# Block-causal attention with a gated convolution FFN: P's transposes read float32r instead of float32, through a second tile that takes over P's bytes, and the planned slot is 10.65 instead of 10.91

## The chip, the cores and the metric

The kernel runs on one core of one Trainium2 chip. The metric is the device time of one execution in microseconds (us), as the median of several runs. The profile is one further execution of the same program, recorded by the hardware profiler; its span runs from the first to the last recorded instruction.

Engines are named as the profile names them: PE is the matrix engine, PEld its weight loads (they run beside PE), DVE the vector engine, ACT the scalar engine, POOL the GpSimd engine, SP the engine that issues most DMAs.

## The reference

Eight sequences of 576 tokens, eight heads of 64 dimensions. Attention is causal by blocks of 64 tokens; its output feeds a feed-forward layer whose hidden values are gated by a convolution over three tokens.

```python
scores = (1/8) * q @ k.T                       # per batch and head, 576 x 576
scores = where(block(i) >= block(j), scores, -1e9)    # blocks of 64
attn = exp(scores - max) ; attn /= sum(attn) + 1e-9
x = concat over heads of attn @ v              # (8, 576, 512)
h = maximum(x @ w_in, 0)                       # (8, 576, 1024)
c[s] = w0*h[s-1] + w1*h[s] + w2*h[s+1]         # per channel
out = (h * sigmoid(c)) @ w_out                 # (8, 576, 512)
```

## The kernel before

**Numbers.** Nearly all matrix products are made with float32r operands, a rounded float32, in three passes: each operand is split into a high part (its rounding) and a low part (the rest), and high by high, high by low and low by high are added in PSUM. Transposes on PE are the exception: they take plain float32 and a float32 identity, `ident`, and only what is evicted from PSUM is split.

**Attention.** Heads go in pairs ("visits"). Batch 0 is visited twice per pair, part A for tokens 0 to 255 and part B for 256 to 575; batches 1 to 7 in one visit per pair, 28 visits in all, part `None`. A visit has two slots, one for each head. For a block of 128 query rows, `stage_s` makes the scores (L930, L932 on PE), the maximum on DVE (L940), the exponential on ACT with its sum (L943), and `finish` the reciprocal on DVE and the normalisation on POOL (`norm`, L859), which multiplies the tile `p0` to `p4` in place by the reciprocal. Parts A and B have their own copies of `norm` (L1072, L1012). The tiles have the widths 128, 256, 384, 512 and 576, two buffers each, and one buffer for `p4`, the last 64 rows of both heads.

**P's transposes.** P stands with queries on the partitions and P times V needs keys there, so `stage_x` transposes P in pieces of 128 columns on PE (`tr` in `one_bank`, L1116): the piece of P is the stationary operand, loaded as weights, and the identity moves through the array. Each call of `one_bank` fills one PSUM bank (`w`) with one to four pieces; ACT evicts the high part (L1126, `ptah` or `ptbh`), DVE the low part (L1129, `ptal` or `ptbl`). In a visit of part `None` there are eight calls with 3, 3, 4, 3, 3, 4, 4 and 1 pieces: 25 transposes. Part A has 2 calls with 3 pieces, part B 6 calls with 19 pieces in all. Together 28 x 25 + 4 x 6 + 4 x 19 = 800 transposes. P times V follows at L1207. Q's and K's transposes (L725) are float32 too.

**FFN.** `ffn` multiplies x by w_in (L1283), runs the convolution and the gate on ACT, DVE and POOL, and multiplies by w_out (L1342). Its matmuls are "paced": they have target times and are laid between the attention work of the next batch.

**The order.** No loop order reaches the engines. The kernel first writes all pieces of work as `Op`s, each with engine, estimated duration, dependencies, buffers and a target time. `Plan.order` then simulates the five engines and fixes the order in which each engine gets its instructions; at run time every engine follows its fixed list and waits on semaphores. Target times of the attention work come from the length of a slot, `SLOT`, 10.91 us in the part `None`; `ffn` takes its pace from `H * SLOT / 2`. A group of n transposes is put at n x 0.109 + 0.003 us. Where the simulated PE would idle longer than a limit, the planner lays in matmuls that compute nothing (`work`, L1473: identity by identity, 512 columns, into a PSUM bank that is free).

Of the kernel before, what the change touches and what calls it, by code (L numbers as in the profile page):

```python
# [9 lines left out]
F32 = mybir.dt.float32  # L10
F32R = mybir.dt.float32r
# [222 lines left out]
def kernel(  # L234
# [10 lines left out]
    nc = tc.nc  # L245
# [81 lines left out]
    def one(shape, dtype, tag):  # L327
        return pl.buf(cp, shape, dtype, tag, 1)
# [514 lines left out]
    def finish(blocks, st, c0, t0, pb, done, exps, part):  # L843
        a, b_, w_ = c0 + blocks[0], c0 + blocks[-1] + 1, 2 if blocks[0] < 4 else 3

        def i1():
            x = 4 if blocks[0] == 4 else 4 + 2 * blocks[0]
            nc.vector.tensor_reduce(out=st.ap[:, a:b_],
                                    in_=st.ap[:, x:x + w_ * (b_ - a)].rearrange("p (n w) -> p n w", w=w_),
                                    op=ALU.add, axis=AX.X)  # L850

        def i2():
            nc.vector.reciprocal(st.ap[:, a:b_], st.ap[:, a:b_])  # L853

        o = pl.op(DVE, 0.15, i1, t0, deps=exps[4] if blocks[0] == 4 else [exps[x] for x in blocks], bufs=[st])
        o = pl.op(DVE, 0.12, i2, t0, deps=[o], bufs=[st])
        for x in blocks:
            def norm(pt=pb[x], col=c0 + x):
                nc.gpsimd.tensor_scalar(out=pt.ap, in0=pt.ap, scalar1=st.ap[:, col:col + 1], scalar2=0.0,  # L859
                                        op0=ALU.mult, op1=ALU.add)  # L860

            w = 128 * (x + 1) if x < 4 else S
            if x in NORMS[part]:
                def norm_a(pt=pb[x], col=c0 + x):
                    nc.scalar.activation(out=pt.ap, in_=pt.ap, func=AF.Copy, scale=st.ap[:, col:col + 1])

                done[x] = pl.op(ACT, c_act(w, False, True), norm_a, t0 + 0.3, deps=[o], bufs=[st, pb[x]])
                continue
            done[x] = pl.op(POOL, c_pool(w) + 0.08, norm, t0 + 0.3, deps=[o], bufs=[st, pb[x]])


    def last_s(t, ready4, t0, pb, done, exps, part):
        st4 = keep([P, 16], F32, "st4", 2, EPS)
        p4 = one([P, S], F32, "p4")
        pb[4] = p4
        ms, es, banks = [], [], []
        for j in range(2):
            k0, k1 = HS * j, HS * j + HS
            sb = bank("s")
            banks.append(sb)  # L880

            def mm4(sb=sb, k0=k0, k1=k1):
                qdh, qdl = t["qz"].ap[:, S - 64:S + 64], t["qdl"].ap
                for n, (q_, k_) in enumerate(((qdh, "kh"), (qdl, "kh"), (qdh, "kl"))):
                    nc.tensor.matmul(sb.ap[:, 0:HS], q_, t[k_].ap[:, k0:k1], start=(n == 0), stop=(n == 2))  # L885

            def mx4(sb=sb, j=j):
                nc.vector.tensor_reduce(out=st4.ap[:, j:j + 1], in_=sb.ap[:, 0:HS], op=ALU.max, axis=AX.X)

            o = pl.op(PE, 3 * c_mm(HS), mm4, t0, deps=ready4, bufs=[sb, t["qz"], t["qdl"], t["kh"], t["kl"]])  # L890
            ms.append(pl.op(DVE, c_dve(HS), mx4, t0 + 0.3, deps=[o], bufs=[sb, st4]))

        def mm4b():
            nc.vector.tensor_reduce(out=st4.ap[:, 2:3], in_=st4.ap[:, 0:2], op=ALU.max, axis=AX.X, negate=True)
# [12 lines left out]

    def stage_s(ops, hh, at, part, shared):
# [52 lines left out]
    def stage_sb(ops, at):  # L961
# [4 lines left out]
        for z, i in enumerate((2, 3)):  # L966
# [16 lines left out]
                      area=0.85, rows64=True)  # L983
            es = []
            for hh in range(2):
                pt = two([P, nk], F32, f"p{i}")
                pb[hh][i] = pt
                j = 2 * z + hh

# [19 lines left out]
            o = pl.op(DVE, 0.13, i2, t0 + 1.2 + OSH, deps=[o], bufs=[st])  # L1009
            for hh in range(2):  # L1010
                def norm(pt=pb[hh][i], col=12 + 2 * z + hh):
                    nc.gpsimd.tensor_scalar(out=pt.ap, in0=pt.ap, scalar1=st.ap[:, col:col + 1], scalar2=0.0,  # L1012
                                            op0=ALU.mult, op1=ALU.add)

                done[hh][i] = pl.op(POOL, c_pool(nk) + 0.08, norm, t0 + 1.5 + OSH + 0.3 * hh, deps=[o], bufs=[st, pb[hh][i]])
        last_s(t, ready4, at + OSB * 2, pb[0], done[0], exps[0], "B")
# [4 lines left out]
    def stage_sa(ops, at):  # L1021
# [1 line left out]

        st = keep([P, 16], F32, "st", 4, EPS)
        sb = [bank("s"), bank("f")]
        pb = [{i: two([P, 128 * (i + 1)], F32, f"p{i}") for i in range(2)} for _ in range(2)]
        done, exps = [{}, {}], []

        def mm(tiles):
# [24 lines left out]
        def ex(hh, i):  # L1054
            def go():
                j = 2 * hh + i
                nc.scalar.activation(out=pb[hh][i].ap, in_=sb[hh].ap[:, 128 * i:128 + 256 * i], func=AF.Exp,
                                     bias=st.ap[:, j:j + 1], accum_out=st.ap[:, 4 + 2 * j:5 + 2 * j])

            return go  # L1060
# [8 lines left out]
        def norm(hh, i):  # L1069
            def go():  # L1070
                j = 12 + 2 * hh + i
                nc.gpsimd.tensor_scalar(out=pb[hh][i].ap, in0=pb[hh][i].ap, scalar1=st.ap[:, j:j + 1], scalar2=0.0,  # L1072
                                        op0=ALU.mult, op1=ALU.add)

            return go

# [23 lines left out]
    def stage_x(pbd, hh, at, part, shared):  # L1100
# [10 lines left out]
        def one_bank(trs, rows, n, hi, lo, deps, t0, bufs_p, bufs_hi, bufs_lo, sub_ok, tag, shape):  # L1111
            tb = bank(tag)

            def tr():
                for z, (x, c, kk, col) in enumerate(trs):
                    nc.tensor.matmul(tb.ap[0:kk, col:col + P], pb[x].ap[:, 128 * c:128 * c + kk], ident,  # L1116
                                     start=(z == 0), stop=True, is_transpose=True, skip_group_check=True)
# [392 lines left out]
```

## Time and profile before

| what | value |
|---|---|
| time, median of 3 runs (lowest to highest) | 806.87 us (806.38 to 807.34) |
| span of the profiled execution | 805.2 us |
| PE busy | 793.4 us, 99% of the span |
| weight loads busy | 712.1 us, 88% |
| DVE, ACT, POOL busy | 649.9, 614.6, 424.1 us |
| granted PE clock, mean | 1.000 |
| P's transposes (L1116): matmuls busy | 125.0 us, 800 of them |
| P's normalisation on POOL (L859): busy | 140.4 us, 256 of them |

The profiled execution has no time of its own beside its span; the median of the runs is 1.7 us above the span, which is what lies ahead of the first and behind the last instruction. Matmuls are recorded from issue to end and overlap each other, so that the recorded mean of one (274 ns for a transpose) is a latency; what one costs PE is the distance to the next.

### The profile page before, as it was taken

The page shows a single profiled execution, that of the slowest core. Times are in us where ns is not written, and L with a number is a line of the kernel's source. Part 1 is how long each engine was busy: PE and PEld are TensorE (multiplying, and loading weights), DVE is VectorE, ACT ScalarE, POOL GpSimd, SP SyncE. Part 2 cuts the span into 40 slices and gives each one's busy share as a digit, 9 for nine tenths or more (in the row PEclk, how much of TensorE's full clock was granted, in tenths as well). Part 3 has the DMA queues.
Part 4 walks back from the last instruction along what each step waited for, and adds up shares of the span by engine and source line. Part 5 has one row for each costly group of instructions (what it writes and reads, how often), then busy time and mean ns, then how long its engine had stood idle before and what let it go on. Part 6 is the DMA issues. An engine that isn't in the chain of part 4 may idle for free.

```text
span 805.2 us, 17261 instructions
## 1 busy us (share of the span) xinstructions
PE 793.4 (99%) x5381; PEld 712.1 (88%) x5381; DVE 649.9 (81%) x1889; ACT 614.6 (76%) x1769; POOL 424.1 (53%) x607
## 2 busy tenths in 40 slices
PE   8999999999999999999999999999999999999998
PEld 5668889888989899898989889898989989899996
DVE  6898989988979779797988869798887959887541
ACT  4769978977968769796978769697877858787652
POOL 3345556666655446565555645555455635546431
PEclk9999999999999999999999999999999999999999
DMA  9423556475445545444455544445554434540001
GB/s 231 143 65 92 144 122 149 111 182 145 104 116 125 134 118 120 110 101 120 120 135 135 122 117 99 102 115 135 135 122 118 110 98 105 136 105 14 14 27 40
DMA packets 163327, 91.35 MB, mean 113 GB/s; under 512 B 134540, under 2 KB 138660, under 8 KB 163236
## 3 DMA queue, kind: packets, MB, share of 16 engines
q1 hardware_dynamic: 162692, 90.12, 45.1%
q8 instruction: 44, 0.72, 0.4%
q14 instruction: 47, 0.39, 0.2%
q10 hardware_dynamic: 544, 0.13, 0.1%
HBM read 38.30 MB, written 9.44 MB: 59 GB/s over the span
## 4 chain that ended last, share of the span: by engine, by line
PE 82%; ACT 6%; DVE 5%; DMA 2%; issue 2%; POOL 2%; SPq 1%; ACTq 0%; POOLq 0%; DVEq 0%
PE f L1283 21%; PE f L1342 19%; PE w L1207 10%; PE w L1116 9%; PE s L930 4%; PE s L932 4%; PE w L1342 3%; PE s L885 3%; PE w L725 3%; PE s L1283 2%; ACT ptbh L1126 1%; DMA vn<-in_v_dram 1%; POOL vv L437 1%; DMA gh<-in_moe_w_in_dram 1%; PE s L1473 1%
## 5 line engine op out<-in xcount | busy, mean ns | idle before, releaser
L859 POOL TENSOR_SCALAR p<-p,st 128x256 f32<-128x256 f32 (+4 forms) x256 | 140.4, 562 | 139.0 <-DVE st L853 82.8
L1323 POOL TENSOR_TENSOR gl<-t,gh 128x288 fp32r<-128x288 f32 (+2 forms) x128 | 104.1, 816 | 148.8 <-ACT gh L1320 145.4
L943 ACT ACTIVATE p<-s,st 128x128 f32<-128x128 f32 x224 | 118.0, 527 | 41.9 <-DVE st L940 40.8
L1116 PE MATMUL w<-ident,p 128*128 128x128 f32 (+1 forms) x800 | 125.0, 274 | 0.7 <-DVE xl L1231 0.3
L940 DVE TENSOR_REDUCE st<-s 128x1 f32<-128x128 f32 x224 | 107.5, 484 | 3.4
L1126 ACT ACTIVATE ptbh<-w 128x384 fp32r<-128x384 f32 (+1 forms) x192 | 93.7, 508 | 21.7 <-PE w L1116 19.2
L1116 PEld LDWEIGHTS w<-ident,p 128*128 128x128 f32 (+1 forms) x800 | 95.0, 139 | 15.5 <-POOL p L859 1.7
L1342 PE MATMUL f<-woh,gh 128*128 128x512 f32 x248 | 103.9, 419 | 0.0
L1283 PE MATMUL f<-xh,wih 128*128 128x290 f32 (+2 forms) x480 | 97.7, 307 | 0.3 <-DVE t L1316 0.3
L1342 PE MATMUL f<-woh,gl 128*128 128x512 f32 x248 | 97.9, 395 | 0.0
L1129 DVE TENSOR_TENSOR ptbl<-w,ptbh 128x512 fp32r<-128x512 f32 (+1 forms) x144 | 89.6, 633 | 10.3 <-ACT ptbh L1126 7.4
L1342 PE MATMUL f<-wol,gh 128*128 128x512 f32 x248 | 97.7, 394 | 0.0
L1283 PE MATMUL f<-xh,wil 128*128 128x290 f32 (+2 forms) x480 | 94.5, 304 | 0.0
L1283 PE MATMUL f<-xl,wih 128*128 128x290 f32 (+2 forms) x480 | 93.3, 304 | 0.0
L1304 DVE SCALAR_TENSOR_TENSOR t<-f,cw,t 128x287 f32<-128x287 f32 (+3 forms) x120 | 59.9, 499 | 19.0 <-ACT t L1300 17.3
L1283 PEld LDWEIGHTS f<-xh,wih 128*128 128x128 f32 x480 | 73.1, 189 | 1.9 <-DVE t L1316 0.5
L1283 PEld LDWEIGHTS f<-xl,wih 128*128 128x128 f32 x480 | 72.9, 189 | 1.0
L1283 PEld LDWEIGHTS f<-xh,wil 128*128 128x128 f32 x480 | 73.2, 189 | 0.4
L932 PE MATMUL s<-kl,qz 128*128 128x128 f32 x224 | 72.1, 322 | 0.0
L1320 ACT ACTIVATE gh<-t 128x288 fp32r<-128x288 f32 (+2 forms) x128 | 56.7, 445 | 8.3 <-DVE t L1316 7.4
L1300 ACT ACTIVATE t<-f,cw 128x288 f32<-128x288 f32 (+2 forms) x120 | 59.9, 499 | 3.8
L1308 DVE SCALAR_TENSOR_TENSOR t<-f,cw,t 128x288 f32<-128x288 f32 (+3 forms) x120 | 60.6, 505 | 1.3
(230 smaller groups left out, 2001.0 us busy)
## 6 DMA issues: line engine op xcount, KB each, us to landing
out_dram<-stage SPq DMA_DIRECT2D x36, 256.0 KB, 2.2
vn<-in_v_dram SPq DMA_DIRECT2D x64, 128.0 KB, 2.9
qn<-in_q_dram SPq DMA_DIRECT2D x56, 144.0 KB, 2.9
kn<-in_k_dram SPq DMA_DIRECT2D x56, 144.0 KB, 3.1
ka<-kh SPq DMA_DIRECT2D x56, 144.0 KB, 2.6
kb<-kh SPq DMA_DIRECT2D x56, 144.0 KB, 2.6
qa<-qh SPq DMA_DIRECT2D x28, 144.0 KB, 2.4
qb<-qh SPq DMA_DIRECT2D x28, 144.0 KB, 2.6
```

Of the source, the lines that this page charges most:

```text
L859: nc.gpsimd.tensor_scalar(out=pt.ap, in0=pt.ap, scalar1=st.ap[:, col:col + 1], scalar2=0.0, op0=ALU.mult, op1=ALU.add)
L932: nc.tensor.matmul(sb.ap[:, 0:nk], qz.ap[:, z:z + 128], kl.ap[:, 0:nk], start=False, stop=True)
L940: nc.vector.tensor_reduce(out=st.ap[:, i:i + 1], in_=sb.ap[:, 0:nk], op=ALU.max, axis=AX.X, negate=True)
L943: nc.scalar.activation(out=pt.ap[:, 0:nk], in_=sb.ap[:, 0:nk], func=AF.Exp, bias=st.ap[:, i:i + 1], accum_out=st.ap[:, 4 + 2 * i:5 + 2 * i])
L1116: nc.tensor.matmul(tb.ap[0:kk, col:col + P], pb[x].ap[:, 128 * c:128 * c + kk], ident, start=(z == 0), stop=True, is_transpose=True, skip_ ...
L1126: nc.scalar.activation(out=hi(), in_=src(), func=AF.Copy)
L1129: nc.vector.tensor_tensor(out=lo(), in0=src(), in1=hi(), op=ALU.subtract)
L1207: nc.tensor.matmul(tb.ap[0:m, q0 - qa:qb - qa], vv.ap[:, chunk(c), hh, w[ps_]], pm.ap[:, 128 * c + q0:128 * c + qb] if qa == 0 else pm.ap[ ...
L1283: nc.tensor.matmul(fb.ap[:, 0:n2], wt[:, c, fs], xs[c][xi].ap[:, x0:x0 + n2], start=(n + c - c0 == 0), stop=(n + c - c0 == 3 * NCC - 1))
L1308: nc.vector.scalar_tensor_tensor(out=t.ap[:, 0:i1], in0=fb.ap[:, own + 1:own + 1 + i1], scalar=cw[:, 2 * NFC + f:2 * NFC + f + 1], in1=t.a ...
L1323: nc.gpsimd.tensor_tensor(out=gbuf[1].ap[:, f, carry:carry + no], in0=t.ap[:, 0:no], in1=gbuf[0].ap[:, f, carry:carry + no], op=ALU.subtract)
L1342: nc.tensor.matmul(fb.ap[:, 0:DM], gbuf[a].ap[:, f, cs], w[:, f, :], start=(f == 0 and n == 0), stop=(f == NFC - 1 and n == 2))
```

## The change

The identity that P's transposes move is now `rident`, the float32r copy that was there already, and P is read as float32r. P itself is still written as float32 by ACT and normalised as float32 by POOL. A new class, `Twin`, holds two tiles under one tag with one buffer: the float32 tile, and a float32r tile that is allocated in the same place once the float32 tile is done with. So that the second tile has a writer, each tile is two columns wider, and a GpSimd memset (`turn`) writes zeros into the two last columns of the float32r tile; the transposes are made to depend on that memset by hand. The two buffers of a tag are now two tags of one buffer each. The bytes that the transposes read are the ones that the normalisation wrote. There is one memset for each normalisation: 28 x 9 + 4 x 4 + 4 x 5 = 288.

The planner's figures change with it: a group of n transposes is put at n x 0.088 + 0.003 us (with `area=0.6` in place of 0.49, the share by which it counts as PE activity), and `SLOT` is 10.65. The memset is not among the planner's `Op`s; it stands in the function of the normalisation.

```diff
+class Twin(Buf):
+    def __init__(self, pool, shape, tag):
+        super().__init__(pool, shape, F32, tag)
+        self.r = None
+
+    @property
+    def raw(self):
+        if self.r is None:
+            pool, shape, _, tag = self.args
+            self.r = pool.tile(shape, F32R, tag=tag, name=tag + "r")
+        return self.r
+
+    def turn(self, nc):
+        n = self.args[1][1]
+        self.set = nc.gpsimd.memset(self.raw[:, n - 2:n].bitcast(F32), 0.0)
...
-    SLOT, SLOTA, SLOTB = 10.91, 3.29, 6.01
+    SLOT, SLOTA, SLOTB = 10.65, 3.29, 6.01
...
+    def twin(nk, tag, n):
+        hist = pl.tags.setdefault(tag, [])
+        b = Twin(cp, [P, nk + 2], f"{tag}{len(hist) % n}")
+        hist.append(b)
+        if len(hist) > n:
+            b.before = hist[-1 - n]
+        return b
...
             def norm(pt=pb[x], col=c0 + x):
-                nc.gpsimd.tensor_scalar(out=pt.ap, in0=pt.ap, scalar1=st.ap[:, col:col + 1], scalar2=0.0,
+                x = pt.ap[:, 0:pt.args[1][1] - 2]
+                nc.gpsimd.tensor_scalar(out=x, in0=x, scalar1=st.ap[:, col:col + 1], scalar2=0.0,
                                         op0=ALU.mult, op1=ALU.add)
+                pt.turn(nc)
...
-            pt = two([P, nk], F32, f"p{i}")
+            pt = twin(nk, f"p{i}_", 2)
...
             def tr():
                 for z, (x, c, kk, col) in enumerate(trs):
-                    nc.tensor.matmul(tb.ap[0:kk, col:col + P], pb[x].ap[:, 128 * c:128 * c + kk], ident,
+                    m = nc.tensor.matmul(tb.ap[0:kk, col:col + P].bitcast(F32R), pb[x].raw[:, 128 * c:128 * c + kk], rident,
                                      start=(z == 0), stop=True, is_transpose=True, skip_group_check=True)
-
-            o = pl.op(PE, len(trs) * 0.109 + 0.003, tr, t0, deps=deps, bufs=[tb] + bufs_p, area=0.49)
+                    tc.add_manual_dep(m.ins, pb[x].set.ins.name, mybir.DependencyInfo(mybir.DependencyClass.Sync, mybir.DependencyReason.DATA), reason="values")
+
+            o = pl.op(PE, len(trs) * 0.088 + 0.003, tr, t0, deps=deps, bufs=[tb] + bufs_p, area=0.6)
```

The same two lines of `norm` stand in `stage_sb` and `stage_sa`. Since the planner's figures changed, each engine's whole order is another. In the rows below a row is line, operation, output<-inputs and size of the output, and xN counts equal neighbours. The lines of the changed kernel stand some 30 further down: L859 is L887 there, L930 and L932 are L959 and L961, L1116 is L1149, L1283 is L1317, L1342 is L1376, L1473 is L1507; the memset is L57.

POOL, one head of a visit in the middle of the program, with buffer numbers; before, four normalisations with one subtraction of the FFN (`gl`) between them, then V's split (`vv`) and the normalisation of `p4`:

```order
L859 TENSOR_SCALAR p0_5526<-p0_5526,st2_101 128x128
L859 TENSOR_SCALAR p1_5549<-p1_5549,st2_101 128x256
L859 TENSOR_SCALAR p2_5565<-p2_5565,st2_101 128x384
L1323 TENSOR_TENSOR gl_1022<-t_5545,gh_1017 128x288
L859 TENSOR_SCALAR p3_5599<-p3_5599,st2_101 128x512
L395 TENSOR_SCALAR vv_5641<-vn_5276 128x10x64
L437 TENSOR_TENSOR vv_5641<-vn_5276,vv_5641 128x10x64
L859 TENSOR_SCALAR p4_5643<-p4_5643,st41_111 128x576
```

The same engine in the changed kernel, at about the same place:

```order
L887 TENSOR_SCALAR p4_0_5935<-p4_0_5935,st41_111 128x576
L57 MEMSET p4_0r_5985 128x2
L422 TENSOR_SCALAR xh_6003<-xt_5744 128x576
L1357 TENSOR_TENSOR gl_1007<-t_5871,gh_998 128x288
L1411 TENSOR_TENSOR xl_6034<-xt_5744,xh_6003 128x576
L1357 TENSOR_TENSOR gl_1007<-t_5960,gh_998 128x288
L887 TENSOR_SCALAR p0_1_5990<-p0_1_5990,st3_103 128x128
L57 MEMSET p0_1r_6114 128x2
L887 TENSOR_SCALAR p1_1_6047<-p1_1_6047,st3_103 128x256
L57 MEMSET p1_1r_6118 128x2
L887 TENSOR_SCALAR p2_1_6085<-p2_1_6085,st3_103 128x384
L57 MEMSET p2_1r_6127 128x2
```

Behind each normalisation stands its memset, which waits for the normalisation's end by a semaphore of POOL itself; transposes wait for the memset.

PE, second half of a slot in the middle of the program; before, scores of 384 and 512 columns, P's transposes and FFN matmuls (`f<-xh,wih` and so on) in turn:

```order
L932 MATMUL s<-kl,qz_105 128x384
L1116 MATMUL w<-ident,p_5903 128x128
L1116 MATMUL w<-ident,p_5910 128x128 x2
L1283 MATMUL f<-xh,wih 128x290 x2
L725 MATMUL w<-ident,kn 128x96 x3
L1283 MATMUL f<-xh,wih 128x290 x2
L930 MATMUL s<-kb,qb 128x512
L932 MATMUL s<-kl,qz_105 128x512
L1116 MATMUL w<-ident,p_5927 128x128 x3
L1283 MATMUL f<-xh,wil 128x290 x2
L1116 MATMUL w<-ident,p_5974 128x128 x4
```

The same place in the changed kernel:

```order
L961 MATMUL s<-kl,qz_105 128x384
L752 MATMUL w<-ident,kn 128x96 x3
L1317 MATMUL f<-xh,wih 128x290 x2
L1149 MATMUL w<-rident,p_0r 128x128 x3
L752 MATMUL w<-ident,kn 128x96 x3
L1317 MATMUL f<-xh,wih 128x290 x2
L959 MATMUL s<-kb,qb 128x512
L961 MATMUL s<-kl,qz_105 128x512
L1149 MATMUL w<-rident,p_0r 128x128 x3
L1317 MATMUL f<-xh,wil 128x290 x4
L1317 MATMUL f<-xl,wih 128x290 x2
L1149 MATMUL w<-rident,p_0r 128x128 x8
```

The transposes keep their place among scores and FFN matmuls, but the groups fall together otherwise: here eight stand in one run where before a run had four.

PE in part B of batch 0, where the planner lays in matmuls that compute nothing; before, four and three of them (`f<-rident`, `w<-rident`):

```order
L1116 MATMUL w<-ident,p_1183 128x128 x3
L1132 MATMUL w<-ptbh,nident 128x512
L1283 MATMUL f<-xl,wih 128x256 x4
L1116 MATMUL w<-ident,p_1368 128x128 x4
L1132 MATMUL w<-ptbh,nident 128x384
L1473 MATMUL f<-rident 128x512 x4
L1116 MATMUL w<-ident,p_1368 64x128
L1473 MATMUL w<-rident 128x512 x3
L1116 MATMUL w<-ident,p_1218 128x128 x3
```

The changed kernel there:

```order
L1149 MATMUL w<-rident,p_0r 128x128 x3
L1166 MATMUL w<-ptbh,nident 128x512
L1317 MATMUL f<-xl,wih 128x256 x4
L1149 MATMUL w<-rident,p_0r 128x128 x4
L1166 MATMUL w<-ptbh,nident 128x384
L1507 MATMUL f<-rident 128x512 x3
L1149 MATMUL w<-rident,p_0r 64x128
L1507 MATMUL s<-rident 128x512 x5
L1149 MATMUL w<-rident,p_1r 128x128 x3
```

Over the whole program there are 117 such matmuls in place of 100, all but four of the 117 ahead of the end of part B.

More of the change, by code (lines that the diff above doesn't have):

```diff
@@ L873, in last_s @@
         st4 = keep([P, 16], F32, "st4", 2, EPS)
-        p4 = one([P, S], F32, "p4")
+        p4 = twin(S, "p4_", 1)
         pb[4] = p4
@@ L985, in stage_sb @@
             for hh in range(2):
-                pt = two([P, nk], F32, f"p{i}")
+                pt = twin(nk, f"p{i}_", 2)
                 pb[hh][i] = pt
@@ L1025, in stage_sa @@
         sb = [bank("s"), bank("f")]
-        pb = [{i: two([P, 128 * (i + 1)], F32, f"p{i}") for i in range(2)} for _ in range(2)]
+        pb = [{i: twin(128 * (i + 1), f"p{i}_", 2) for i in range(2)} for _ in range(2)]
         done, exps = [{}, {}], []
@@ L1056, in go @@
                 j = 2 * hh + i
-                nc.scalar.activation(out=pb[hh][i].ap, in_=sb[hh].ap[:, 128 * i:128 + 256 * i], func=AF.Exp,
+                nc.scalar.activation(out=pb[hh][i].ap[:, 0:128 * (i + 1)], in_=sb[hh].ap[:, 128 * i:128 + 256 * i], func=AF.Exp,
                                      bias=st.ap[:, j:j + 1], accum_out=st.ap[:, 4 + 2 * j:5 + 2 * j])
@@ L1071, in go @@
                 j = 12 + 2 * hh + i
-                nc.gpsimd.tensor_scalar(out=pb[hh][i].ap, in0=pb[hh][i].ap, scalar1=st.ap[:, j:j + 1], scalar2=0.0,
+                x = pb[hh][i].ap[:, 0:128 * (i + 1)]
+                nc.gpsimd.tensor_scalar(out=x, in0=x, scalar1=st.ap[:, j:j + 1], scalar2=0.0,
                                         op0=ALU.mult, op1=ALU.add)
+                pb[hh][i].turn(nc)
             return go
```

4 lines of the change are left out of this document (3 added, 1 removed).

## The prediction

> **What bounds the kernel now.** I read the page's busy times first, then the stretches of the span, then the chain that ended last, then the single weight loads.
>
> ```profile
> span 805.2 us, 17261 instructions
> PE 793.4 (99%) x5381; PEld 712.1 (88%) x5381; DVE 649.9 (81%) x1889; ACT 614.6 (76%) x1769; POOL 424.1 (53%) x607
> ```
>
> A busy PE is not yet a full PE, so the stretches count more. Each row: stretch, its length, then busy us of PE, weight loads, DVE, ACT and POOL.
>
> ```profile
> core 0: us, PE busy (x) PEld busy (x) DVE busy (x) ACT busy (x) POOL busy (x), PEclk, DMA share, GB/s
> 60.00:130.00 70.00, 69.37 (x514) 60.69 (x513) 62.12 (x179) 62.56 (x178) 39.17 (x62) 1.00 0.51 129
> 250.00:400.00 150.00, 149.84 (x1043) 138.33 (x1042) 126.00 (x371) 118.52 (x345) 80.78 (x114) 1.00 0.47 115
> 400.00:550.00 150.00, 149.85 (x1038) 137.71 (x1037) 126.01 (x371) 119.17 (x349) 83.59 (x115) 1.00 0.49 119
> ```
>
> From 60 us on PE is never free for more than about 1% (69.37 of 70), in the middle for 0.1% (149.84 of 150), at the full granted clock, while DVE has 16% to spare. So PE is the bound, and what a matmul costs there is its distance to the next one. The chain that ended last gives that distance for the transposes: start, length, what.
>
> ```profile
> 502.47 0.69 PE f L1342 x3
> 503.16 0.87 PE w L1116 x8
> 504.74 0.11 PE w L1116
> ```
>
> Eight transposes hold PE for 0.87 us, a single one for 0.11: **0.109 us each**, twice what 128 moving columns need elsewhere. A 512-column float32r matmul follows the one before it after 0.23 and 0.22 us, so that 128 such columns take 0.225 / 4 = 0.056 us:
>
> ```profile
> 405.95 0.39 PE L1342 MATMUL f<-woh,gh 128*128 128x512 f32 x1
> 406.18 0.39 PE L1342 MATMUL f<-wol,gh 128*128 128x512 f32 x1
> 406.40 0.40 PE L1342 MATMUL f<-woh,gl 128*128 128x512 f32 x1
> ```
>
> With weights it is the other way round. Mean length of one load is the number behind the comma; the 128x128 and 128x64 in each row are the weights.
>
> ```profile
> L1116 PEld LDWEIGHTS w<-ident,p 128*128 128x128 f32 x768 | 91.9, 140 | 15.1 <-POOL p L859 1.7 <-POOL p L1072 1.0 <-DVE ptbl L1129 0.8
> L1116 PEld LDWEIGHTS w<-ident,p 128*64 128x64 f32 x32 | 3.5, 111 | 0.4
> L1283 PEld LDWEIGHTS f<-xh,wih 128*128 128x128 f32 x480 | 73.1, 189 | 1.9 <-DVE t L1316 0.5 <-DVE st L894 0.2
> L1207 PEld LDWEIGHTS w<-ptbl,vv 128*64 128x64 f32 x256 | 26.8, 136 | 0.9
> ```
>
> Going from 64 to 128 columns adds 140 - 111 = 29 ns to a transpose's float32 load and 189 - 136 = 53 ns to a float32r load. So 128 columns take about 0.058 us in the first and 0.106 us in the second, the rest is fixed. Where float32r matmuls are short, their loads pace them: here three loads start 0.11 us apart, behind matmuls of 128 columns.
>
> ```profile
> 401.25 0.19 PEld L930 LDWEIGHTS s<-kb,qb 128*128 128x128 f32 x1
> 401.36 0.19 PEld L932 LDWEIGHTS s<-kl,qz 128*128 128x128 f32 x1
> 401.47 0.30 PEld L1283 LDWEIGHTS f<-xl,wih 128*128 128x128 f32 x2
> ```
>
> Today's transpose thus loads fast (0.058) and moves slowly (0.109); a plain float32r product of the same size would move fast (0.056) and load slowly (0.11). A step is the longer of the two. What a float32r transpose does, no row shows: it is either 0.058 or about 0.11 us, and that decides the case.
>
> **The change, part by part.**
>
> *The transposes.* Moving at 0.056 us I take as given, since every float32r row does it. For the load the ends are 0.058 us (it goes with the operation) and 0.11 us (it goes with the type). I take 0.058: that row is the same piece of P, in the same transposing form, and only the name of the type differs. Affected are the transposes in stretches where PE is full:
>
> ```profile
> L1116 PE MATMUL w<-ident,p x800: 270/272/332, 14.2 to 739.2; 128*128 128x128 f32 x154, 128*64 128x128 f32 x6
> ```
>
> The same line by stretches, matmuls and loads with their counts:
>
> ```profile
> core 0: us, PE busy (x) PEld busy (x), PEclk, DMA share, GB/s
> 0.00:60.00 60.00, 4.78 (x27) 3.13 (x27) 1.00 0.56 147
> ```
>
> 27 of 800 lie ahead of 60 us, which leaves 773. They save 773 x (0.109 - 0.058) = 39.4 us. Part of it comes back behind each run: the next float32r weights need 0.11 us to load, and the last transpose now covers 0.058 of it. The kernel makes 8 calls in each of 28 visits and 6 in each of 4, so at most 248 runs, x 0.052 = 12.9 us. Net: **-26.5 us**, and nothing if the load goes with the type.
>
> *What is late next.* With 26.5 us less PE work, DVE's 84% become 87%. The stretch from 60 to 130 us shows what such a load does: DVE at 62.12 of 70 (89%), and PE lost 0.9% there against 0.1% in the middle. I give back 0.8% of 700 us: **+5.6 us** (between 0 and that row's rate).
>
> *The memsets.* 288 of them on POOL. A memset of 128x1 took 98 ns there, and a POOL instruction that waits for the one before it by semaphore starts about 0.08 us late (286.20 + 0.73 = 286.93, next start 287.02).
>
> ```profile
> L1494 POOL MEMSET const-float32-0.0<- 128x1 f32 x1 | 0.1, 98 | 0.2 <-issue 0.2
> 283.10 2.05 POOL L859 TENSOR_SCALAR p<-p,st 128x128 f32<-128x128 f32 x4 [8.60 <-ACT stage L1352]
> 286.20 0.73 POOL L395 TENSOR_SCALAR vv<-vn 128x640 fp32r<-128x640 f32 x1 [1.05 <-issue]
> 287.02 1.58 POOL L437 TENSOR_TENSOR vv<-vn,vv 128x640 fp32r<-128x640 f32 x1
> ```
>
> That is 0.18 us each and 52 us on POOL, 424 to 476, still under 60% of the span. But each P is ready 0.18 us later, and the last of four 0.72 us later (2.05 becomes 2.8). Behind a memset in POOL's fixed order stand the next normalisation, the FFN's subtraction (`gl`), for which the w_out matmuls wait, and the splits of V and x, for which P times V and the w_in matmuls wait. Today's transposes hardly wait for POOL (total us, times):
>
> ```profile
>   POOL p L859: 1.9, 7
>   POOL p L1072: 1.0, 4
> ```
>
> 11 waits, 2.9 us. I let that nearly double, **+2.5 us**; ends 0 (all hidden under PE's other work) and the rival below.
>
> *The idle matmuls.* 17 more, at 0.225 us 3.8 us, laid where the planner sees PE idle, in parts A and B. They are free if it is idle there and cost all if it isn't; the stretch from 60 to 130 says nearly full, the start not. Half: **+1.9 us**.
>
> *The slot.* 10.65 shortens no instruction; it only changes the order and is already in the runs counted above. Wider P tiles (two columns) are not read by anyone: 0.
>
> Sum on the profiled execution: 805.2 - 26.5 + 5.6 + 2.5 + 1.9 = 788.7 us. Runs take 1.7 us more than the span (806.87 against 805.2): **790.4 us**, 2.0% faster. Rounded 790.
>
> **The rivals.**
>
> *No gain: the load goes with the type.* Then a step is 0.11 us in place of 0.109, whichever way the identity moves. For it speaks that every float32r load of 128 columns here is 187 to 190 ns long (the 189 above), with no exception, and that no row has a float32 load that isn't a transpose, so form and type can't be told apart. Time: 806.9, plus 773 x 0.001 = 0.8 for the step, plus up to 3.8 for idle matmuls: 806.5 to 811. The same comes out if the change doesn't do what it says, that is if the float32r name leaves a transpose as it was (step 0.109, loads of 140 ns).
>
> The Trainium skill (TensorE: Matmul & The Clock Gate, section LDWEIGHTS) has a rule that speaks for this rival: a weight load takes its columns divided by 1.2 GHz, whatever the rows, which is 107 ns for 128 columns. The trace agrees with it for float32r loads (0.11 us apart) and not for today's transposes, whose 128 columns cost 0.058 us; by the rule the time would stay at 807, by the rows of L1116 it falls.
>
> *Slower: POOL becomes late.* One mechanism: the memset at the end of each normalisation delays P by 0.18 to 0.72 us, and PE, in its fixed order, stands still at the first transpose of a run. At a delay of two results (0.36 us) 53 of the 248 runs would have to wait to eat up the gain of 16.5 us and the 2.5 us already counted; with every third run waiting (83) it costs 30 us in place of the 2.5, and the time is 790.4 - 2.5 + 30 = 818. Against it: POOL is 53% busy, idles 8.6 us ahead of the four normalisations quoted above, and 11 waits are few. For it: the planner doesn't count the memset, so the order leaves no room for it.
>
> *More: nothing comes back.* If DVE, POOL and the idle matmuls cost nothing, 805.2 - 26.5 + 1.7 = 780.4; and if runs stand together more often (as the run of eight does), fewer loads are exposed and it may be a few us less.
>
> **How the numbers follow.** The forecast, with its own range of 780 to 798, has 0.60. No gain has 0.26; half of it lies within 0.2% of 806.9 (about what a measurement of this kernel can tell from no change) and half above. POOL late has 0.08, on the slow side. More than 26.5 us has 0.06. So faster 0.66, same 0.13, slower 0.21. The range takes the forecast with its lower bound, 780.4 less about one, and reaches up into the no-gain case to 809; left out are its upper part, POOL late, and the larger gains, together about 0.2. Range 779 to 809.
>
> **What would show it.** Right: P's loads stay near 140 ns and runs of eight transposes take about 0.47 us in the chain in place of 0.87, with the weights behind them waited for. Load by type: loads of 189 ns and 0.11 us a transpose. Name without effect: 140 ns and 0.109. DVE's part: PE's busy share in the middle falls from 99.9% towards 99%. POOL late: waits of PE or its loads for POOL's memset of tens of us instead of 2.9. The forecast is wrong if a step lies between 0.058 and 0.109, which no row here would explain, or if PE's fixed order makes it wait for an engine that has time on average.

## The result, and the profile after

| | median | runs | lowest to highest |
|---|---|---|---|
| before | 806.81 us | 4 | 806.38 to 807.34 |
| changed | 817.45 us | 4 | 816.05 to 818.69 |

The ratio is **1.0131**, 95% interval 1.0117 to 1.0145: the changed kernel is 1.3% slower, 10.6 us, where 2.0% faster was forecast. The page of the changed kernel gives its span and the busy time of each engine, then the chain that ended last:

```profile
span 815.9 us, 17504 instructions
PE 791.0 (97%) x5398; PEld 705.5 (86%) x5398; DVE 647.7 (79%) x1889; ACT 611.0 (75%) x1769; POOL 456.2 (56%) x895
...
PE 76%; POOL 9%; DVE 5%; ACT 5%; issue 2%; DMA 1%; SPq 0%; ACTq 0%; POOLq 0%
```

PE's busy time fell by 2.4 us while the span grew by 10.7: PE now stands still. POOL, only 56% busy, holds 9% of the chain; it was 2% before. The stretches of the changed kernel, in the columns of those of before:

```profile
core 0: us, PE busy (x) PEld busy (x) DVE busy (x) ACT busy (x) POOL busy (x), PEclk, DMA share, GB/s
60.00:130.00 70.00, 64.17 (x458) 55.11 (x458) 57.98 (x159) 56.47 (x159) 39.94 (x82) 0.95 0.42 107
...
250.00:400.00 150.00, 149.67 (x1063) 137.54 (x1062) 125.03 (x371) 117.48 (x347) 92.61 (x182) 1.00 0.50 120
400.00:550.00 150.00, 148.34 (x1050) 136.30 (x1049) 125.77 (x374) 117.31 (x348) 85.90 (x168) 1.00 0.49 119
```

The worst row is the first. From 60 to 130 us PE does 458 matmuls where before it did 514, 5.83 us of the 70 are idle, and the granted clock is 0.95. In the middle PE gets through more matmuls than before (1063 against 1043), but it is no longer full (148.34 of 150).

What P's transposes wait for, and for how long, in the changed kernel (total us, times):

```profile
  POOL p_0r L57: 19.0, 30
  POOL p_1r L57: 5.2, 13
```

That is 43 waits and 24.2 us for the memset (L57), against 11 waits and 2.9 us for the normalisation before: "waits of PE or its loads for POOL's memset of tens of us", the sign that the prediction had set for its slow rival. This view adds the idle time of PE and that of its weight loads, which wait for the same P, so a stall can count twice. PE's own part, as the largest group of it before and then after (total us, times, longest):

```profile
PE w L1116 <- POOL p L859: 0.2, 1, 0.2
```

```profile
PE w L1149 <- POOL p_0r L57: 7.8, 14, 2.7
```

With 1.3 us in 4 waits for `p_1r`, PE alone waits 9.1 us for the memset, where it waited 0.2 us for the normalisation before.

The transposes themselves did become faster. First a run of eight in before's timeline of matmuls (start, length, what), with the matmul that follows; then one in the changed kernel:

```profile
503.00 1.04 PE L1116 MATMUL w<-ident,p 128*128 128x128 f32 x8
503.79 0.48 PE L1342 MATMUL f<-woh,gh 128*128 128x512 f32 x1
```

```profile
258.48 0.81 PE L1149 MATMUL w<-rident,p_0r 128*128 128x128 f32 x8
259.13 0.50 PE L1317 MATMUL f<-xl,wih 128*128 128x290 f32 x2
```

From the first start to the next matmul's it is 0.79 us before and 0.65 after: 0.14 us for a run of eight. By the prediction it should have been 8 x 0.051 - 0.052 = 0.36. The prediction had set its sign in the chain that ended last, 0.47 us for eight in place of 0.87; there it is 0.65, and a single transpose with 64 columns of weights takes 0.06 in place of 0.11:

```profile
258.65 0.65 PE w L1149 x8
259.63 0.06 PE w L1149
```

The loads of the same run, in the timeline of weight loads:

```profile
258.39 0.76 PEld L1149 LDWEIGHTS w<-rident,p_0r 128*128 128x128 f32 x8
259.09 0.30 PEld L1317 LDWEIGHTS f<-xl,wih 128*128 128x128 f32 x2
```

Eight loads take 0.70 us, 0.0875 each, though a single one is still 140 ns long. So the load goes with the operation and not with the type, as forecast, but a step is neither 0.058 nor 0.11: it lies near 0.086.

Three questions are open at this point: what the float32r transposes gain alone, what the memsets cost, and what the new planner's figures cost.

### The profile page after: what moved, and what is told of

Same layout as the page of the kernel before. It is cut to its first block, busy times and chain, and to the rows that moved or that the text cites. A ratio compares the mean times of both kernels' runs of the same rounds, so it can differ in the third digit from the quotient of the medians.

```text
span 815.9 us, 17504 instructions
## 1 busy us (share of the span) xinstructions
PE 791.0 (97%) x5398; PEld 705.5 (86%) x5398; DVE 647.7 (79%) x1889; ACT 611.0 (75%) x1769; POOL 456.2 (56%) x895
## 4 chain that ended last, share of the span: by engine, by line
PE 76%; POOL 9%; DVE 5%; ACT 5%; issue 2%; DMA 1%; SPq 0%; ACTq 0%; POOLq 0%
PE f L1317 20%; PE f L1376 18%; PE w L1241 10%; PE w L1149 6%; PE s L959 4%; PE s L961 4%; PE w L1376 3%; PE w L752 3%; PE s L914 2%; POOL p L887 2%; PE s L1317 2%; POOL vv L464 1%; DMA ka<-kh 1%; POOL xl L1411 1%; POOL vv L422 1%
## 5 line engine op out<-in xcount | busy, mean ns | idle before, releaser
L887 POOL TENSOR_SCALAR p<-p,st 128x256 f32<-128x256 f32 (+4 forms) x256 | 144.7, 565 | 115.2 <-DVE st L880 58.3
L1160 ACT ACTIVATE ptbh<-w 128x384 fp32r<-128x384 f32 (+1 forms) x192 | 91.0, 508 | 36.8 <-PE w L1149 36.1
L1376 PE MATMUL f<-woh,gh 128*128 128x512 f32 x248 | 103.5, 417 | 0.0
L1376 PE MATMUL f<-woh,gl 128*128 128x512 f32 x248 | 97.9, 395 | 0.0
L1376 PE MATMUL f<-wol,gh 128*128 128x512 f32 x248 | 97.9, 395 | 0.0
L1317 PE MATMUL f<-xl,wih 128*128 128x290 f32 (+2 forms) x480 | 97.5, 307 | 0.0
L1317 PE MATMUL f<-xh,wih 128*128 128x290 f32 (+2 forms) x480 | 96.3, 308 | 0.4 <-DVE t L1350 0.4
L1317 PE MATMUL f<-xh,wil 128*128 128x290 f32 (+2 forms) x480 | 89.6, 303 | 0.0
L1317 PEld LDWEIGHTS f<-xh,wih 128*128 128x128 f32 x480 | 73.8, 191 | 3.3 <-DVE t L1350 0.6
L1317 PEld LDWEIGHTS f<-xl,wih 128*128 128x128 f32 x480 | 73.8, 191 | 1.1
L1317 PEld LDWEIGHTS f<-xh,wil 128*128 128x128 f32 x480 | 72.7, 191 | 0.4
L961 PE MATMUL s<-kl,qz 128*128 128x128 f32 x224 | 72.2, 322 | 0.0
L1149 PEld LDWEIGHTS w<-rident,p_0r 128*128 128x128 f32 (+1 forms) x480 | 51.8, 139 | 19.4 <-POOL p_0r L57 11.2
L1149 PE MATMUL w<-rident,p_0r 128*128 128x128 f32 (+1 forms) x480 | 58.9, 242 | 8.0 <-POOL p_0r L57 7.8
L1347 ACT ACTIVATE t<-t 128x288 f32<-128x288 f32 (+2 forms) x128 | 57.1, 446 | 10.4 <-DVE t L1342 9.8
L1342 DVE SCALAR_TENSOR_TENSOR t<-f,cw,t 128x288 f32<-128x288 f32 (+3 forms) x120 | 60.6, 505 | 1.2
```

Source lines behind the costliest of these rows:

```text
L887: nc.gpsimd.tensor_scalar(out=x, in0=x, scalar1=st.ap[:, col:col + 1], scalar2=0.0, op0=ALU.mult, op1=ALU.add)
L961: nc.tensor.matmul(sb.ap[:, 0:nk], qz.ap[:, z:z + 128], kl.ap[:, 0:nk], start=False, stop=True)
L1149: m = nc.tensor.matmul(tb.ap[0:kk, col:col + P].bitcast(F32R), pb[x].raw[:, 128 * c:128 * c + kk], rident, start=(z == 0), stop=True, is_t ...
L1160: nc.scalar.activation(out=hi(), in_=src(), func=AF.Copy)
L1317: nc.tensor.matmul(fb.ap[:, 0:n2], wt[:, c, fs], xs[c][xi].ap[:, x0:x0 + n2], start=(n + c - c0 == 0), stop=(n + c - c0 == 3 * NCC - 1))
L1376: nc.tensor.matmul(fb.ap[:, 0:DM], gbuf[a].ap[:, f, cs], w[:, f, :], start=(f == 0 and n == 0), stop=(f == NFC - 1 and n == 2))
```

## The experiments

Each ratio is to the kernel before, timed on the same chip beside it (medians of before 806.39, 807.18 and 806.31 us in the three groups of four, 806.81 for the changed kernel), with its 95% interval. Differences in us between runs of different groups carry up to 0.9 us of these medians.

### Group 1: the parts apart

**t1**: the changed kernel with the planner's old figures.

```diff
-    SLOT, SLOTA, SLOTB = 10.65, 3.29, 6.01
+    SLOT, SLOTA, SLOTB = 10.91, 3.29, 6.01
...
-            o = pl.op(PE, len(trs) * 0.088 + 0.003, tr, t0, deps=deps, bufs=[tb] + bufs_p, area=0.6)
+            o = pl.op(PE, len(trs) * 0.109 + 0.003, tr, t0, deps=deps, bufs=[tb] + bufs_p, area=0.49)
```

> The changed kernel with the planner's old figures (0.109 us a transpose, area 0.49, slot 10.91), so that the order is that of before; float32r transposes and memsets stay. Theory O (the new order costs the time: it is planned without the memsets and with a shorter slot): about 795, faster than before, because the step of a transpose fell from 0.109 to 0.085 us in the changed kernel's trace (700 x 0.024 = 17 us less, some 5 given back). Theory M (the memsets at the end of POOL's chain cost it in any order, waits of PE for them were 24 us in the changed kernel): 808 to 818, not faster than before. Theory L (what the transposes save comes back in the weight loads behind them): about 806.

**t2**: the kernel before with the new figures, and nothing else of the change (the diff of t1 the other way round).

> The kernel before with the planner's new figures (0.088 us a transpose, area 0.6, slot 10.65) and nothing else: float32 transposes, no memset. Theory O: slower than before, 812 to 822, most of it in batch 0. Theory M: 805 to 809, since an order alone costs nothing and PE still has the same work. Theory L: 805 to 809 as well.

**t3**: the kernel before, in its old order, with P's tiles of type float32r; no second tile, no memset. P is rounded here, as it is in t4, t5, t6 and t10.

```diff
-            pt = two([P, nk], F32, f"p{i}")
+            pt = two([P, nk], F32R, f"p{i}")
...
-                    nc.tensor.matmul(tb.ap[0:kk, col:col + P], pb[x].ap[:, 128 * c:128 * c + kk], ident,
+                    nc.tensor.matmul(tb.ap[0:kk, col:col + P].bitcast(F32R), pb[x].ap[:, 128 * c:128 * c + kk], rident,
```

> Float32r transposes without memsets, in the old order: P's exponentials and the normalised P are written as float32r, so P is rounded and its low part is lost, and no second tile is needed. Beside t1 it has everything but the memsets. Theory O: about 793, as t1 or some 2 us below it. Theory M: 790 to 795, with t1 12 us or more above it. Theory L: about 806, as t1.

**t4**: t3 with the new figures (0.088, 0.6, 10.65).

> As t3, P rounded and no memsets, but with the planner's new figures (0.088, 0.6, slot 10.65). Beside the changed kernel it has everything but the memsets. Theory O: 808 to 817, near the changed kernel. Theory M: 788 to 793, about 25 us below the changed kernel, since the order then fits what PE does. Theory L: 806 or more.

| | old figures | new figures |
|---|---|---|
| float32 transposes | 806.39 (before) | t2 815.96; 1.0123 (1.0106 to 1.0140) |
| float32r, no memset | t3 798.73; 0.9908 (0.9893 to 0.9922) | t4 804.26; 0.9975 (0.9964 to 0.9987) |
| float32r with memset | t1 811.83; 1.0072 (1.0055 to 1.0088) | changed 817.45; 1.0131 (1.0117 to 1.0145) |

Read along the columns, the float32r transposes gain 7.7 us in the old order and 11.7 in the new one. The memsets cost 13.1 us in the old (811.8 - 798.7) and 13.2 in the new (12.6 by the ratios); these two rows also differ in the second tile and in P being rounded, so "memsets" stands for all that the second tile brings. Read along the rows, the new figures cost 9.6 us with float32 transposes, 5.5 with float32r ones and 5.6 with memsets (4.8 by the ratios). Along one path, 806.4 - 7.7 + 13.1 + 5.6 = 817.4: two parts of the change lose more than twice what the third gains. The sum closes by construction, and the parts don't add freely: the figures cost 9.6 us as the first step and 5.6 as the last.

The expectations were right in sign more than in size. t1 lies within theory M's range and t2 within O's, but t3 came out between them and theory L's 806, and t4 lies in no theory's range.

Where the new figures lose their time is shown by the first output written. This is the source view of the line that evicts outputs, for before, t3 and t2 in this order; the times behind the lengths are the first and last start:

```profile
L1352 ACT ACTIVATE stage<-f x31: 587/597/614, 121.7 to 748.0; 128x512 f32<-128x512 f32 x31
```

```profile
L1352 ACT ACTIVATE stage<-f x31: 587/598/614, 121.0 to 740.7; 128x512 f32<-128x512 f32 x31
```

```profile
L1352 ACT ACTIVATE stage<-f x31: 587/597/619, 132.3 to 756.6; 128x512 f32<-128x512 f32 x31
```

In t2 the first output is 10.6 us late and the last of these 31 is 8.6: everything is lost ahead of the first output, in parts A and B of batch 0 and what is laid behind them, and a little is won back later. In t3 the first is 0.7 us early and the last 7.3: the transposes' gain accrues in batches 1 to 7.

### Group 2: which figure, and what makes a memset dear

**t5** is t3 with the new 0.088 and 0.6 but the old slot, **t6** is t3 with the new slot alone.

> As t3 (P rounded, float32r transposes, no memsets), slot 10.91, but the planner counts a transpose at 0.088 us and area 0.6. It splits the 5.5 us that lie between t3 (798.7) and t4 (804.3). Theory C (the shorter transposes rearrange parts A and B, where t2 and t4 were 10.6 and 11.2 us behind at the first output): 803 to 812, with the first output some 10 us later than in t3. Theory S (the slot does it): 797 to 800, first output as in t3 (121.6 us).

> As t3, with the planner's old figures for a transpose (0.109 us, area 0.49) and the slot at 10.65. Theory C: 792 to 799, first output as in t3 (121.6 us), because the slot touches batches 1 to 7 alone. Theory S: 803 to 812.

t5 took 802.30 us, 0.9941 (0.9926 to 0.9956); t6 799.71, 0.9907 (0.9893 to 0.9922), which is t3 again. Both lie just outside theory C's ranges, but on its side by the first output, below. It is the group's figures that lose, not the slot. (On top of them the slot costs some 0.3%: t4 against t5.) The same line of t5:

```profile
L1352 ACT ACTIVATE stage<-f x31: 587/599/632, 132.7 to 743.5; 128x512 f32<-128x512 f32 x31
```

Its first output comes 11.7 us after t3's, its last only 2.8 after: from the first to the last, t5 is 8.9 us quicker than t3. **The same figures harm batch 0 and help batches 1 to 7.** The harm can be seen in t5's timeline of matmuls and in its stretches around it:

```profile
81.32 0.75 PE L1116 MATMUL w<-rident,p 128*128 128x128 f32 x4 [2.54 <-POOL p L1012]
```

```profile
core 0: us, PE busy (x) PEld busy (x) DVE busy (x) ACT busy (x) POOL busy (x), PEclk, DMA share, GB/s
76.00:80.00 4.00, 2.66 (x21) 2.09 (x18) 3.75 (x12) 3.95 (x14) 3.24 (x7) 1.00 0.26 57
80.00:84.00 4.00, 2.68 (x12) 2.25 (x14) 1.87 (x6) 1.60 (x5) 2.83 (x4) 0.63 0.46 103
84.00:88.00 4.00, 4.00 (x22) 3.44 (x21) 2.44 (x5) 2.00 (x6) 0.73 (x1) 0.52 0.79 248
88.00:92.00 4.00, 4.00 (x37) 3.71 (x38) 1.86 (x7) 3.57 (x11) 1.05 (x2) 1.00 0.05 17
```

PE stands 2.54 us for a normalisation, up to 81.32 us, and its clock reads 0.63 and 0.52 in the two rows from 80 us. In stretches of 1 us it is 0.52 from 81, 0.50 from 82 to 87, 0.57 from 87 and 1.00 from 88 us. PE is busy for 0.68 us of the first of these and all of the others, so that about 3.3 us of work are lost. A busy PE hides this: the row from 84 us reads 4.00 of 4, with 22 matmuls where the next one has 37. Stall and clock are 5.8 of the 11.7 us; the rest, elsewhere ahead of the first output, was not broken down. t2 and t4 have the same stall, 2.5 us, and 0.67 and 0.90, and 0.65 and 0.50, in the rows from 80 us; in t3, without it, the clock is 1.00 in all four rows. The changed kernel has it too, 2.67 us up to 83.19, and 0.84, 0.50 and 0.80 in the rows from 80 us on. It also stands 2.07 us for a DMA (`ka<-kh`) up to 586.54, with a clock of 0.58 from 588 to 592 us. The Trainium skill (TensorE: Matmul & The Clock Gate, Part 1) says that the clock drops to half after an idle window of about 3.4 us. The half rate agrees with the 0.50; here, though, a gap of 2.54 us was enough.

**t7** is t1 with two one-column memsets for each normalisation in place of one of two columns; in **t8** (also t1) the memsets stay, but the transposes wait for the normalisation and no longer for the memset behind it.

```diff
-        self.set = nc.gpsimd.memset(self.raw[:, n - 2:n].bitcast(F32), 0.0)
+        nc.gpsimd.memset(self.raw[:, n - 2:n - 1].bitcast(F32), 0.0)
+        self.set = nc.gpsimd.memset(self.raw[:, n - 1:n].bitcast(F32), 0.0)
```

```diff
-                nc.gpsimd.tensor_scalar(out=x, in0=x, scalar1=st.ap[:, col:col + 1], scalar2=0.0,
+                pt.nrm = nc.gpsimd.tensor_scalar(out=x, in0=x, scalar1=st.ap[:, col:col + 1], scalar2=0.0,
...
-                    tc.add_manual_dep(m.ins, pb[x].set.ins.name, mybir.DependencyInfo(mybir.DependencyClass.Sync, mybir.DependencyReason.DATA), reason="values")
+                    tc.add_manual_dep(m.ins, pb[x].nrm.ins.name, mybir.DependencyInfo(mybir.DependencyClass.Sync, mybir.DependencyReason.DATA), reason="values")
```

> As t1 (float32r transposes, memsets, old order), with two memsets of one column behind each normalisation in place of one of two columns; the second need not wait for the first. A result is late by 0.28 us in place of 0.18. Theory M1 (what the memsets cost grows with the time by which P is late; t1 stands 13.1 us above t3): 811.8 + 13.1 x 0.10 / 0.18 = 819, within 3 us. Theory M2 (the wait of POOL for itself, or the second tile as such, costs it, not the length): 811 to 813.

> As t1, but the transposes wait for the normalisation itself and not for the memset behind it. The memsets stay and POOL has as much to do; a P is no longer late by its own memset, only by those of the results ahead of it on POOL (0 to 0.54 us in place of 0.18 to 0.72). Theory M1 (lateness of P): the mean delay of a group of four falls from 0.45 to 0.27 us, so 13.1 x 0.27 / 0.45 = 8 us above t3, 807. Theory M3 (POOL's added work delays what else it does, the FFN's subtraction and the splits): 811 to 812, no change against t1.

t7 took 814.11 us, 1.0078 (1.0059 to 1.0098), within its interval the same as t1, and inconclusive, because the dose was much smaller than meant. A memset in t1's timeline of POOL, with its neighbours:

```profile
289.37 0.10 POOL L57 MEMSET p_0r<- 128x2 f32 x1
289.49 0.59 POOL L887 TENSOR_SCALAR p<-p,st 128x384 f32<-128x384 f32 x1
290.14 0.10 POOL L57 MEMSET p_0r<- 128x2 f32 x1
290.28 0.70 POOL L887 TENSOR_SCALAR p<-p,st 128x512 f32<-128x512 f32 x1
```

The normalisation of 384 columns ends at 290.08 and its memset at 290.24, so that this P is free 0.16 us later; the next normalisation starts at 290.28. Four in a row, 2.05 us before, take 2.86 us here (288.28 to 291.14), 0.20 us more each. The pair of memsets in t7:

```profile
291.44 0.10 POOL L57 MEMSET p_0r<- 128x1 f32 x1
291.48 0.10 POOL L58 MEMSET p_0r<- 128x1 f32 x1
291.58 0.70 POOL L888 TENSOR_SCALAR p<-p,st 128x512 f32<-128x512 f32 x1
```

The second starts 0.04 us after the first, and four normalisations in a row take 2.89 us here (289.58 to 292.47). So the length of a memset costs next to nothing; what costs is either the wait of POOL for its own result or the second tile as such, and t7 doesn't tell these apart.

t8 took 808.49 us, 1.0018 (1.0009 to 1.0028), nearer to theory M1's 807 than to M3's 811. Not waiting for one's own memset is worth 1.0072 - 1.0018, or 4.4 us of the 13.1; the waits of the transposes for POOL fall with it from 23.3 us in t1 to these:

```profile
  POOL p L887: 11.7, 26
  POOL p L1104: 4.7, 9
```

The other two thirds stay. A likely reason is that a memset delays the next normalisation too, and all that stands behind it in POOL's fixed order; t12 tests that.

### Group 3: repair

**t9** is t1 with 0.16 us more in the planner's figure for every normalisation (`c_pool(w) + 0.08` becomes `+ 0.24`, at all three places), so that the order knows of the memset.

> As t1 (float32r transposes, memsets, old figures for transposes and slot), but the planner counts each normalisation on POOL 0.16 us longer, which is what two normalisations in a row took more in t1's trace (their distance beyond their length went from -0.025 to +0.135 us). Theory P (what hurts is that the order leaves no room for the memsets): 800 to 806, 6 us or more below t1's 811.8. Theory Q (POOL's result is late in whatever order, or a changed order costs batch 0 as much as t5's did): 810 to 820.

t9 took 810.80 us, 1.0062 (1.0044 to 1.0081): a miss. That the planner knows of the memsets brought nothing that can be told from t1. It also reorders batch 0, where figures had just been shown to do harm, so that a gain later may be lost there, and the stretches of t1 and, below them, of t9 show this:

```profile
core 0: us, PE busy (x) PEld busy (x) DVE busy (x) ACT busy (x) POOL busy (x), PEclk, DMA share, GB/s
130.00:250.00 120.00, 117.14 (x814) 104.28 (x813) 104.91 (x320) 97.24 (x287) 76.94 (x153) 1.00 0.54 126
250.00:740.00 490.00, 483.58 (x3394) 440.61 (x3393) 409.53 (x1204) 385.90 (x1127) 290.26 (x564) 1.00 0.48 116
```

```profile
130.00:250.00 120.00, 116.54 (x807) 103.72 (x805) 103.14 (x316) 95.02 (x282) 74.66 (x153) 1.00 0.54 127
250.00:740.00 490.00, 486.41 (x3430) 445.44 (x3429) 413.24 (x1222) 388.68 (x1142) 292.56 (x568) 1.00 0.48 117
```

From 250 us on t9 gets through 36 matmuls more than t1, and its transposes' waits for POOL are 5.8 us in place of 23.3. Ahead of that it is behind: 7 matmuls fewer from 130 to 250 us, although 8 of its 807 compute nothing, and 128 such matmuls in the whole program in place of 100. The first output doesn't show it (120.5 us, in t1 125.1); what stands ahead of that output depends on the order. t12 leaves parts A and B as they were.

**t10** is t3 with the new group figures only for batches 1 to 7 (`early` is true in parts A and B), slot 10.91:

```diff
-            o = pl.op(PE, len(trs) * 0.109 + 0.003, tr, t0, deps=deps, bufs=[tb] + bufs_p, area=0.49)
+            o = pl.op(PE, len(trs) * (0.109 if early else 0.088) + 0.003, tr, t0, deps=deps, bufs=[tb] + bufs_p, area=0.49 if early else 0.6)
```

> As t5 (P rounded, no memsets, slot 10.91), but 0.088 us and area 0.6 only in the visits of batches 1 to 7; parts A and B keep 0.109 and 0.49. t5 was 11.7 us behind t3 at the first output and 2.7 us at the last but one, so it made good 9 us in batches 1 to 7. Theory C2 (the loss is the new order of parts A and B alone, the gain behind it is real): first output near 122, end 798.7 - 9 = 790, within 3 us. Theory C3 (t5 only caught up with its own delay): 797 to 800, as t3.

t10 took **791.31 us, 0.9814** (0.9797 to 0.9830): 11.0 us under t5 and 7.4 under t3. Batch 0 is as good as in t3 (first output 120.8 us against 121.0), batches 1 to 7 as good as in t5 (610.8 us from the first output to the last in both). Its outputs and its middle:

```profile
L1352 ACT ACTIVATE stage<-f x31: 584/598/625, 120.8 to 731.6; 128x512 f32<-128x512 f32 x31
```

```profile
core 0: us, PE busy (x) PEld busy (x) DVE busy (x) ACT busy (x) POOL busy (x), PEclk, DMA share, GB/s
250.00:400.00 150.00, 150.00 (x1068) 138.75 (x1067) 128.78 (x387) 123.09 (x362) 86.89 (x120) 1.00 0.49 121
400.00:550.00 150.00, 150.00 (x1053) 137.37 (x1052) 126.27 (x375) 119.75 (x347) 81.20 (x116) 1.00 0.50 122
```

**t11** is t8 (memsets kept, P in full float32) with the split figures of t10. **t12** is t11 with the 0.16 us of t9 counted, but only in batches 1 to 7:

```diff
-            done[x] = pl.op(POOL, c_pool(w) + 0.08, norm, t0 + 0.3, deps=[o], bufs=[st, pb[x]])
+            done[x] = pl.op(POOL, c_pool(w) + (0.08 if part else 0.24), norm, t0 + 0.3, deps=[o], bufs=[st, pb[x]])
```

> An exact version for use, P not rounded: as t8 (float32r transposes, memsets, transposes wait for the normalisation) with the figures of t10, 0.088 us and area 0.6 in batches 1 to 7, 0.109 and 0.49 in parts A and B, slot 10.91. Theory C2: 808.5 - 9 = 800, faster than the kernel before by some 0.8%. Theory C3, or memsets that eat up the gain there: 806 to 809.

> As t11, and the planner counts each normalisation of batches 1 to 7 0.16 us longer, for its memset; parts A and B are left as they are. Theory P: 2 to 5 us below t11. Theory Q: at t11 or above it.

t11 took 805.18 us, 0.9985 (0.9976 to 0.9994), a miss in size: the split figures bring 0.33% here against t8, where they brought 0.94% without memsets (t10 against t3). A tighter order of PE seems to be worth little as long as P comes late. t12 took **798.17 us, 0.9895** (0.9881 to 0.9910): 7.0 us under t11, by nothing but 0.16 us that the planner counts, and more than the 2 to 5 expected. The waits of the transposes for POOL in t12:

```profile
  POOL p L1104: 4.8, 10
  POOL p L887: 4.1, 10
```

8.9 us, against 17.2 in t11. t12 is the fastest kernel here that keeps P as it was, 1.05% under the kernel before. Against t10 it still lacks 6.9 us; its first output is 3.8 us later (124.6 against 120.8), where the planner still doesn't count the memsets.

## Why the prediction was wrong, step by step

- **PE is the bound: right.** Where PE is full, faster transposes pay at once: in the middle of t10 it does 25 matmuls more in 150 us than before (1068 against 1043).
- **Load by operation: right. The step of 0.058: mis-sized.** The loads stayed at 140 ns and are 0.0875 us apart, a step "between 0.058 and 0.109", which the prediction had named as a sign of being wrong. It is the load that sets this step, not the move. Behind a transpose with 64 columns of weights, which moves the same 128 columns of the identity, the next load starts 0.06 us later (t3):

```profile
520.71 0.11 PEld L1116 LDWEIGHTS w<-rident,p 128*64 128x64 f32 x1
520.77 0.30 PEld L1283 LDWEIGHTS f<-xh,wih 128*128 128x128 f32 x2
```

So 64 columns more cost about 0.03 us, as the prediction had it. But it took the fixed part of a load, found from loads of 64 and 128 columns, to be hidden completely, and some 0.03 us of it isn't. With a step of 0.085 its own formula gives 773 x 0.024 - 248 x 0.025 = 12.4 us in place of 26.5. The runs without memsets give 7.7 (t3, old order) and 15.0 (t10, split figures). The Trainium skill's rule on loads (TensorE: Matmul & The Clock Gate, LDWEIGHTS), by estimate 107 ns for 128 columns, holds for the other float32r loads (0.11 us apart) and not for these.
- **DVE late, +5.6: not there in t10,** where PE is full (150.00 of 150) with DVE at 86%. A little of it shows in t3, in the old order: PE at 149.31 of 150 from 250 to 400 us, and DVE with 15% of the chain that ended last, 5% before.
- **Memsets, "+2.5": the first step that failed; 13.1 us.** The price of one was right (0.18 us forecast, 0.16 to 0.20 measured), and POOL stayed under 60% busy (56%). What was wrong is "I let that nearly double": lateness was judged by the waits before, 11 of them, which don't say by how much P was early. (PE itself had 0.2 of those 2.9 us, its weight loads the rest.) PE's order is fixed, so a P that is 0.16 to 0.81 us later can make PE stand, the other sign of being wrong that the prediction had named. For lateness that the order doesn't allow for, and against POOL's capacity, speaks t12: with POOL doing the same work as in t11, room for 0.16 us in the order brings 7.0 us, and the waits halve; t9 shows the same from 250 us on. That another order was better by accident is not excluded, since no other figure was tried.
- **The figures, "only changes the order": the second step that failed; 5.5 to 9.6 us.** The sum has no term for them. For the slot alone that was right in the old order (t6). For 0.088 and 0.6, whose price the prediction doesn't mention, it was wrong: they rearrange parts A and B, PE stands 2.5 us, the clock is halved behind that, and the first output is 11 us late. Split by batch the same figures gain 7.4 us (t10 against t3). Which of the two figures does it was not separated. The idle matmuls (+1.9) lie in the same parts; their cost was not separated either.
- **The rivals.** "POOL late" was the mechanism of the larger loss, and its 818 us is near the 817.45, but partly by chance: it put 27.5 us more on POOL against a gain of 26.5. Both were about twice too large, and the order had no part in it. It had a chance of 0.08; the prediction had itself named a reason for more, a memset that the planner doesn't count. "No gain" rested on float32r loads of 187 to 190 ns "with no exception"; the means of their groups in the kernel before start at 182 ns, which changes nothing in the argument.

What stays open: the 6.9 us between t12 and t10, what the second tile costs apart from its memset, and whether a marker on another engine than POOL would be free. None of these was tried.

## What to carry to other kernels

- When a simulated planner fixes the order at build time, its cost figures are part of the kernel. Try new figures alone, without the change that they describe (t2), and ask of each stage whether they suit it: the same 0.088 and 0.6 lost 11 us in one stage and gained 8.9 in the others.
- A tiny instruction at the end of a dependency chain costs its latency at each consumer that was just in time, however idle its engine is on average. Few waits before are no slack; slack is how long the data lay ready, and what the planner doesn't count it leaves no room for.
- A small grid (operation by order, with and without the marker) tells in four runs which of several parts that cancel is worth keeping; its steps depend on the path, so read more than one.

## What the runs showed of the hardware

- A float32r transpose of 128 columns has a step of about 0.086 us: between the float32 one (0.109) and the plain float32r load (0.11) on one side and the move of 128 float32r columns (0.056) on the other. Its load lasts 140 ns; other float32r loads last 189. With 64 columns of weights the step is 0.06 us, so the load sets it.
- A stall of PE of 2.54 us went with some 7 us at a granted clock of about 0.5 (t5). The clock cost more (3.3 us) than the stall. The length of a gap alone doesn't decide: after one of 1.04 us (t7, up to 605.15 us) the clock read 0.63 from 606 to 610 us, after one of 1.06 us (before, at 598.6 us) it stayed at 1.00.
- A memset on POOL that waits for POOL's own result lets its reader go 0.16 us later and lengthens a row of normalisations by 0.20 us each; a second one right behind it starts 0.04 us after the first.
